# The second half of a decode kernel's result accumulated in another quadrant of the PE array

## The chip, the cores and the metric

The kernel runs on one core of one Trainium2 chip. The metric is the device time of one execution in microseconds (us). Three runs of the kernel before took 129.09 to 129.24 us, the median is 129.13 us. One further execution was recorded by the hardware profiler; all lines of profile come from such executions. Engines are named as in the profile: PE is TensorE (PEld its weight loads), DVE is VectorE, ACT ScalarE, POOL GpSimd, and SPq the queue of SyncE, which issues the large DMA transfers.

## The reference

One token (a row `x` of 576 values) goes through a parallel block: attention over a sliding window of a cache, and a gated MLP, both on the normalised row, and both added to `x`:

```python
def _A_ref(x, k_cache, v_cache, wq, wo):
    W = min(4096, max(256, Sk // 4))                     # 4096
    q = (x @ wq) ...                                     # 32 heads of 128
    k = jnp.repeat(k_cache[:, :, Sk - W:, :], rep, axis=1)   # 16 kv heads, rep = 2
    v = jnp.repeat(v_cache[:, :, Sk - W:, :], rep, axis=1)
    scores = jnp.einsum('bhqd,bhkd->bhqk', q, k) * Dh ** (-0.5)
    p = _softmax(scores, axis=-1)
    o = jnp.einsum('bhqk,bhkd->bhqd', p, v)
    return o... @ wo                                     # 4096 x 576

def _B_ref(x, w_in, w_sp, b_sp, w_out):
    z = _gelu(jnp.einsum('bsd,df->bsf', x, w_in))        # 576 x 4608
    z1 = z[..., :Fh].copy()
    z2 = _layernorm(z[..., Fh:], axis=-1)
    g = jnp.einsum('ts,bsf->btf', w_sp, z2) + b_sp[None, :, None]
    return jnp.einsum('bsf,fd->bsd', z1 * g, w_out)      # 2304 x 576

xn = _layernorm(x, axis=-1)
return x + _A_ref(xn, ...) + _B_ref(xn, ...)
```

All tensors are bf16. Some 51 MB are read: 16 heads of 4096 rows of K and of V (33.6 MB), `wq`, `w_in`, `w_out` and `wo`.

## The kernel before

All large reads are issued by SyncE at the head of the program, in the order in which they are used, into a ring of seven buffers: `wq` in two pieces, then K and V in pairs of heads with `w_in` between, then `w_out` (one piece, `wout` in the profile) and last `wo` in six pieces of 10, 8, 6, 4, 2 and 2 rows, a row being 128 x 576 values. A transfer into a buffer of the ring waits until what it held has been used; for the last pieces of `wo` that is the attention's product with V.

The order on each engine is the order of the program; no scheduler moves instructions. The steps:

- The row is normalised and spread (`XT`), and `wq` is applied in four quadrants of the PE array (L208, `qps`). A quadrant is a strip of 32 columns of the array, and it writes the corresponding 32 partitions of PSUM. `tile_position=(0, 32 * g)` chooses it. Without this argument a matmul with a single column of weights uses the strip at 0.
- For each of the 16 heads, VectorE transposes K (`kT`, L248) and TensorE makes the scores (`S`, L256). Four heads make a group, one quadrant for each head. A group's softmax (`sm_a`, `sm_b`: `mx`, `p`, `pt`, `PT`) and its product with V (`pv`, L306, into `ops`, four heads in four quadrants) come while the next group's scores are made.
- `yb` turns `ops` into the group's columns of `Y` (`om`, L316; `on`, L320; four small fp32 matmuls into `yps`, L323; the cast to `Y`, L327).
- The MLP's first half (`z_mms`, `z_rest`, `z_norm`) lies among the first groups and leaves its result in `hv`.
- The result is accumulated in two PSUM tiles `acc0` and `acc1`, 288 columns each, in a bank of their own. They are begun with `x` itself (L396, two matmuls over one row). `out_mms` (L407) adds one row of `w_out` or `wo`: for each half a weight load of one column of `hv` or `Y` and a matmul over 288 columns.

At the end of the program, behind the last product with V, stand 12 rows of `w_out`, the last group's `yb`, 6 more rows of `w_out`, and the 32 rows of `wo`. The first matmul on each piece waits for its transfer. Then VectorE casts the first half of the result (L427) and ScalarE the second (L428), both into `res`, and SyncE stores it (L429).

Of the kernel before, what the change touches and what calls it, by code (L numbers as in the profile page):

```python
# [8 lines left out]
FP32 = mybir.dt.float32  # L9
# [5 lines left out]
D = 576  # L15
# [14 lines left out]
CW = D // 2  # L30
# [9 lines left out]
def kernel(  # L40
# [14 lines left out]
    nc = tc.nc  # L55
    P = nc.NUM_PARTITIONS
# [10 lines left out]
    ps_a = ctx.enter_context(tc.tile_pool(name="ps_a", bufs=1, space=bass.MemoryType.PSUM))  # L67
    ps_b = ctx.enter_context(tc.tile_pool(name="ps_b", bufs=1, space=bass.MemoryType.PSUM))
# [45 lines left out]
    xrow = const.tile([1, D], BF16, name="xrow")  # L114
# [14 lines left out]
    ones_b = const.tile([1, P], BF16, name="ones_b")  # L129
# [28 lines left out]
    for n in range(2):  # L158
        t = ps_s.tile([P, 2, 512], FP32, name=f"S{n}")
# [46 lines left out]
    for s, wv in wq_sb:  # L206
        for g in range(4):
            nc.tensor.matmul(  # L208
                qps[32 * g:32 * g + 2, :], lhsT=XT[:, s, :], rhs=wv[:, 512 * g:512 * (g + 1)],
                start=(s == 0), stop=(s == NS - 1), tile_position=(0, 32 * g),  # L210
# [12 lines left out]
    for k in range(4):  # L223
        for be in range(4):
            nc.tensor.matmul(
                qps2[:, k, be, :].rearrange("p (r g) -> p r g", r=2),
                lhsT=q_rep[0:NR, 2 * k + be // 2, be % 2].rearrange("p a d -> p (a d)"),
                rhs=idq, start=True, stop=True)
# [14 lines left out]
    def t_head(j):  # L243
        kT = ktpool.tile([P, NT, 2, 32, 2], BF16, name=f"kT{j}", tag="kT")
        src = K[j].rearrange("p t d -> p (t d)").bitcast(FP32)
        dst = kT[:].rearrange("p t b k e -> p (t b k e)").bitcast(FP32)
        for hf in range(2):
            nc.vector.transpose(dst[:, 1024 * hf:1024 * (hf + 1)], src[:, 1024 * hf:1024 * (hf + 1)])  # L248
        KT[j] = kT

    def s_head(j):
        g, i = divmod(j, GK)
        kv = KT.pop(j)[:].rearrange("p t b k e -> p b e t k")
        for hf in range(2):
            for be in range(4):
                nc.tensor.matmul(  # L256
                    S[g % 2][32 * i:32 * i + 8, hf, :],
                    lhsT=Qb[:, j, be].rearrange("p a h -> p (a h)"),
                    rhs=kv[:, be // 2, be % 2, 16 * hf:16 * hf + 16, :],
                    start=(be == 0), stop=(be == 3), tile_position=(0, 32 * i),  # L260
                )
# [13 lines left out]
    def sm_a(g):  # L275
        s = S[g % 2]
        nc.vector.tensor_reduce(out=mx[:, 0:1], in_=s[:], op=ALU.max, axis=mybir.AxisListType.XY)  # L277
        bk = spread(mx, mb, g, ALU.max, "m")
        nm = work.tile([P, 1], FP32, name=f"nm{g}", tag="nm")
        nc.vector.tensor_scalar_mul(nm[:], bk[:, 0:1], -SCALE)  # L280
        p = work.tile([P, 1024], BF16, name=f"p{g}", tag="p")
        nc.scalar.activation(p[:], s[:].rearrange("p a n -> p (a n)"), ACT.Exp, bias=nm[:, 0:1], scale=SCALE,  # L282
                             accum_out=lx[:, 0:1])
        st[g] = {"p": p}

    def sm_b(g):
        d = st[g]
        pt = work.tile([P, NT, 32], BF16, name=f"pt{g}", tag="pt")
        nc.vector.transpose(pt[:].rearrange("p t x -> p (t x)"), d["p"][:])  # L289
        lbk = spread(lx, lb, g, ALU.add, "l")  # L290
        rs = work.tile([P, 1], FP32, name=f"rs{g}", tag="rs")
        nc.vector.reciprocal(rs[:], lbk[:, 0:1])
        PT = work.tile([P, GK, NT, 2], BF16, name=f"PT{g}", tag="PT")
        pt4 = pt[:].rearrange("p t x -> p (t x)").bitcast(FP32).rearrange("p (t x) -> p t x", x=16)
        PT4 = PT[:].rearrange("p i t h -> p (i t h)").bitcast(FP32).rearrange("p (i t) -> p i t", i=GK)
        for i in range(GK):
            for a in range(4):
                nc.scalar.copy(PT4[32 * a:32 * a + 32, i, :], pt4[32 * i:32 * i + 32, :, a])  # L298
        d["PT"] = PT
        d["rs"] = rs  # L300
# [29 lines left out]
    def z_mms():  # L330
        zps = ps_a.tile([P, 2, NF], FP32, name="zps", tag="a")
        for s, wv in win_sb:
            wt = wv.rearrange("k (p t) -> k t p", t=NF)
            for t in range(NF):
                nc.tensor.matmul(zps[:, :, t], lhsT=wt[:, t, :], rhs=XT[:, s, :],  # L335
                                 start=(s == 0 and t == 0), stop=(s == NS - 1 and t == NF - 1),
                                 skip_group_check=True)
        return zps

    def z_rest(zps):  # L340
        z = const.tile([P, 2, NF], FP32, name="z")
        nc.vector.tensor_copy(z[:], zps[:])
        u = const.tile([P, 2, NF], FP32, name="u")
        nc.vector.tensor_mul(u[:], z[:], z[:])
        nc.vector.tensor_scalar(out=u[:], in0=u[:], scalar1=0.044715, scalar2=1.0,
                                op0=ALU.mult, op1=ALU.add)
        nc.vector.tensor_mul(u[:], u[:], z[:])
        th = const.tile([P, 2, NF], FP32, name="th")
        nc.scalar.activation(th[:], u[:], ACT.Exp, scale=-2.0 * GELU_C)
        nc.vector.tensor_scalar_add(th[:], th[:], 1.0)  # L350
        nc.vector.reciprocal(th[:], th[:])
        G = const.tile([P, 2, NF], FP32, name="G")
        nc.vector.tensor_mul(G[:], th[:], z[:])
        sz = const.tile([P, 2], FP32, name="sz")
        nc.vector.reduce_sum(sz[:, 0:1], G[:, 1], axis=AXX)
        jz = const.tile([P, NF], FP32, name="jz")
        nc.vector.tensor_tensor_reduce(
            out=jz[:], in0=G[:, 1], in1=G[:, 1], scale=1.0, scalar=0.0,
            op0=ALU.mult, op1=ALU.add, accum_out=sz[:, 1:2],
        )  # L360
        return G, sz

    def z_norm(G, sz):
        psz = ps_m.tile([P, 512], FP32, name="psz", tag="m")
        nc.tensor.matmul(psz[:, 0:2], lhsT=ones_f[:], rhs=sz[:], start=True, stop=True)
        mz = const.tile([P, 4], FP32, name="mz")
        nc.vector.tensor_scalar_mul(mz[:, 0:2], psz[:, 0:2], 1.0 / FH)
        nc.vector.tensor_mul(mz[:, 2:3], mz[:, 0:1], mz[:, 0:1])
        nc.vector.tensor_sub(mz[:, 2:3], mz[:, 1:2], mz[:, 2:3])
        nc.vector.tensor_scalar_add(mz[:, 2:3], mz[:, 2:3], EPS)  # L370
        nc.gpsimd.tensor_tensor(out=mz[:, 3:4], in0=mz[:, 2:3], in1=mhalf[:], op=ALU.pow)
        zn = const.tile([P, NF], FP32, name="zn")
        nc.vector.tensor_scalar(out=zn[:], in0=G[:, 1], scalar1=mz[:, 0:1], scalar2=mz[:, 3:4],
                                op0=ALU.subtract, op1=ALU.mult)
        nc.vector.tensor_scalar(out=zn[:], in0=zn[:], scalar1=wb[:, 0:1], scalar2=wb[:, 1:2],  # L375
                                op0=ALU.mult, op1=ALU.add)
        hv = const.tile([P, NF], BF16, name="hv")
        nc.vector.tensor_mul(hv[:], G[:, 0], zn[:])
        return hv

    for j in range(HKV):
        t_head(j)
        g, o = divmod(j, GK)
        if g > 0 and o == 0:
            sm_a(g - 1)
        if g > 0 and o == 1:
            sm_b(g - 1)
        s_head(j)
        if j == GK - 1:
            zps = z_mms()  # L390
        if j == GK + 1:
            G, sz = z_rest(zps)

            acc = [ps_a.tile([1, 512], FP32, name="acc0", tag="a"), ps_b.tile([1, 512], FP32, name="acc1")]
            for n in range(2):
                nc.tensor.matmul(acc[n][:, 0:CW], lhsT=ones_b[:, 0:1], rhs=xrow[:, CW * n:CW * (n + 1)],  # L396
                                 start=True, stop=False)
        if j == GK + 2:
            hv = z_norm(G, sz)
        if g > 1 and o == 0:  # L400
            yb(g - 2)
        if g > 0 and o == 3:
            pv(g - 1)

    def out_mms(lhs, col, wv, last):
        for n in range(2):
            nc.tensor.matmul(acc[n][:, 0:CW], lhsT=lhs[:, col:col + 1], rhs=wv[:, CW * n:CW * (n + 1)],  # L407
                             start=False, stop=last)

    def out_hv(c):  # L410
        for t, wv in wout_sb[6 * c:6 * c + 6]:
            out_mms(hv, t, wv, False)
# [10 lines left out]
    for t, wv in wo_sb:  # L423
        out_mms(Y, t, wv, t == 31)

    res = const.tile([1, D], BF16, name="res")
    nc.vector.tensor_copy(res[:, 0:CW], acc[0][:, 0:CW])  # L427
    nc.scalar.copy(res[:, CW:D], acc[1][:, 0:CW])  # L428
    nc.sync.dma_start(out.flatten_outer_dims(), res[:])  # L429


# [28 lines left out]
```

## Time and profile before

| what | us |
|---|---|
| median of three runs | 129.13 |
| lowest and highest | 129.09, 129.24 |
| profiled execution | 129.18 |
| its span, first to last instruction | 127.4 |
| TensorE busy (share of the span) | 79.6 (62%) |
| VectorE busy | 74.0 (58%) |
| ScalarE busy | 23.3 (18%) |
| output matmuls on `wo` (64), busy together, each | 8.0, 0.286 |
| output matmuls on `wout` (36), busy together, each | 4.6, 0.286 |

50.96 MB are read from memory, 400 GB/s over the span. The mean granted clock of TensorE is 0.786 of full speed. In the page's rows of slices, each digit is a fortieth of the span (3.2 us) in tenths; in rows of groups, the numbers behind the bar are busy time in us, the mean duration of one instruction in ns, and the idle time before them. Matmuls are pipelined, so the starts of two may be closer than the duration of one.

### The profile page before, as it was taken

How to read it: one execution, taken by the hardware profiler on the slowest of the kernel's cores; microseconds unless marked ns; L12 is line 12 of the kernel's file. 1: busy time of each engine (PE TensorE's matmuls, PEld its weight loads, DVE VectorE, ACT ScalarE, POOL GpSimd, SP SyncE). 2: the span in 40 equal slices, each digit the busy share in tenths (PEclk: the TensorE clock that was granted, in tenths of full speed). 3: DMA queues.
4: the chain of work that ended last, by engine and by line, in shares of the span. 5: the costliest groups of instructions: out<-in, count | busy, mean ns of one | idle time of the engine just before them, and what ended most of it. 6: DMA issues, size and time to landing. Idle time of an engine off the chain costs nothing.

```text
span 127.4 us, 1582 instructions
## 1 busy us (share of the span) xinstructions
PE 79.6 (62%) x610; PEld 37.2 (29%) x610; DVE 74.0 (58%) x155; ACT 23.3 (18%) x77; POOL 3.6 (3%) x19
## 2 busy tenths in 40 slices
PE   0002911599999697509179653995579703889992
PEld 0001301133899512002123210232112201247660
DVE  6704147999000599463598699998999656050001
ACT  1200030000000003920000307403074059000001
POOL 4301000000000000000100000000000000000000
PEclk9999995558975555555955999679769995599999
DMA  4999999999999999999999999999999999999920
GB/s 135 437 416 427 412 427 432 443 434 421 434 408 432 422 419 430 427 430 427 427 430 427 430 427 430 422 424 430 427 427 430 424 461 452 396 408 429 407 107 0
DMA packets 6174, 51.04 MB, mean 401 GB/s; under 512 B 534, under 2 KB 536, under 8 KB 1048
## 3 DMA queue, kind: packets, MB, share of 16 engines
q1 hardware_dynamic: 6082, 50.96, 94.9%
q8 instruction: 4, 0.07, 0.2%
q10 hardware_dynamic: 86, 0.00, 0.0%
q14 instruction: 2, 0.02, 0.0%
HBM read 50.96 MB, written 0.00 MB: 400 GB/s over the span
## 4 chain that ended last, share of the span: by engine, by line
issue 40%; DMA 27%; PE 21%; DVE 9%; POOLq 0%; POOL 0%; ACT 0%; SPq 0%
DMA wout<-in_B_w_out_dram 20%; PE acc L407 10%; PE S L256 7%; DMA x<-in_A_x_dram 7%; DVE kT L248 4%; PE ops L306 3%; DVE pt L289 1%; DVE on L320 1%; DVE om L316 1%; PE ps_x L185 0%; POOLq L455 0%; PE yps L323 0%; POOL mv L191 0%; ACT res L428 0%; DVE zn L375 0%
## 5 line engine op out<-in xcount | busy, mean ns | idle before, releaser
L256 PE MATMUL S<-kT,Qb 128*8 128x512 bf16 x128 | 42.0, 507 | 20.9 <-DVE kT L248 20.3
L248 DVE STREAM_TRANSPOSE kT<-k 128x1024 f32<-128x1024 f32 x32 | 37.0, 1212 | 11.2 <-DMA k<-in_A_k_cache_dram 11.2
L256 PEld LDWEIGHTS <-Qb 128*8 128x8 bf16 x128 | 12.1, 101 | 46.6 <-issue 38.9
L298 ACT COPY PT<-pt 32x32 f32<-32x32 f32 x64 | 15.4, 241 | 14.3 <-DVE pt L289 13.4
L306 PE MATMUL ops<-v,PT 128*8 128x512 bf16 x128 | 15.0, 497 | 0.4 <-ACT PT L298 0.4
L282 ACT ACTIVATE p<-S,nm 128x1024 bf16<-128x1024 f32 x4 | 4.5, 1114 | 54.5 <-DVE nm L280 54.5
L335 PEld LDWEIGHTS <-win 128*128 128x128 bf16 x162 | 10.1, 171 | 0.4 <-issue 0.4
L335 PE MATMUL zps<-XT,win 128*128 128x2 bf16 x162 | 10.2, 202 | 0.0
L407 PE MATMUL acc<-wo,Y 128*1 128x288 bf16 x64 | 8.0, 286 | 0.0
L323 PE MATMUL yps<-on,sel 128*32 128x32 f32 x32 | 1.9, 209 | 8.5 <-DVE on L320 8.5
L306 PEld LDWEIGHTS <-PT 128*8 128x8 bf16 x128 | 4.4, 93 | 6.5 <-issue 3.7
L407 PEld LDWEIGHTS <-Y 128*1 128x1 bf16 x64 | 5.4, 84 | 2.5
L175 PE MATMUL ps_x<-x,rmat 64*128 64x9 bf16 x1 | 0.2, 165 | 9.4 <-DMA x<-in_A_x_dram 9.4
L277 DVE TENSOR_REDUCE mx<-S 128x1 f32<-128x1024 f32 x4 | 4.9, 1214 | 1.4 <-PE S L256 1.4
L316 DVE SCALAR_TENSOR_TENSOR om<-ops,rs,dmask 128x512 f32<-128x512 f32 x4 | 3.0, 744 | 4.6 <-PE ops L306 4.6
L427 DVE CAST res<-acc 1x288 bf16<-1x288 f32 x1 | 0.4, 447 | 8.9 <-PE acc L407 8.9
L289 DVE STREAM_TRANSPOSE pt<-p 128x1024 bf16<-128x1024 bf16 x4 | 4.8, 1210 | 1.4 <-ACT p L282 1.4
L407 PE MATMUL acc<-wout,hv 128*1 128x288 bf16 x36 | 4.6, 286 | 0.6 <-DMA wout<-in_B_w_out_dram 0.6
L323 PEld LDWEIGHTS yps<-on,sel 128*32 128x32 f32 x32 | 1.5, 122 | 10.0 <-DVE on L320 8.4
L320 DVE TENSOR_REDUCE on<-om 128x128 f32<-128x512 f32 x4 | 4.1, 1024 | 0.1
L208 PE MATMUL qps<-wq,XT 128*2 128x512 bf16 x36 | 3.5, 561 | 0.7 <-DVE XT L199 0.7
L407 PEld LDWEIGHTS <-hv 128*1 128x1 bf16 x36 | 3.1, 85 | 2.4 <-issue 1.2
(89 smaller groups left out, 35.5 us busy)
## 6 DMA issues: line engine op xcount, KB each, us to landing
k<-in_A_k_cache_dram SPq DMA_DIRECT2D x8, 2048.0 KB, 23.5
v<-in_A_v_cache_dram SPq DMA_DIRECT2D x8, 2048.0 KB, 20.5
win<-in_B_w_in_dram SPq DMA_DIRECT2D x3, 1728.0 KB, 22.4
wout<-in_B_w_out_dram SPq DMA_DIRECT2D x1, 2592.0 KB, 25.7
wq<-in_A_wq_dram SPq DMA_DIRECT2D x1, 2560.0 KB, 8.7
wq<-in_A_wq_dram SPq DMA_DIRECT2D x1, 2048.0 KB, 12.9
wo<-in_A_wo_dram SPq DMA_DIRECT2D x1, 1440.0 KB
wo<-in_A_wo_dram SPq DMA_DIRECT2D x1, 1152.0 KB
```

What stands on the lines that cost most here:

```text
L208: nc.tensor.matmul(qps[32 * g:32 * g + 2, :], lhsT=XT[:, s, :], rhs=wv[:, 512 * g:512 * (g + 1)], start=(s == 0), stop=(s == NS - 1), tile ...
L248: nc.vector.transpose(dst[:, 1024 * hf:1024 * (hf + 1)], src[:, 1024 * hf:1024 * (hf + 1)])
L256: nc.tensor.matmul(S[g % 2][32 * i:32 * i + 8, hf, :], lhsT=Qb[:, j, be].rearrange("p a h -> p (a h)"), rhs=kv[:, be // 2, be % 2, 16 * hf ...
L277: nc.vector.tensor_reduce(out=mx[:, 0:1], in_=s[:], op=ALU.max, axis=mybir.AxisListType.XY)
L282: nc.scalar.activation(p[:], s[:].rearrange("p a n -> p (a n)"), ACT.Exp, bias=nm[:, 0:1], scale=SCALE, accum_out=lx[:, 0:1])
L289: nc.vector.transpose(pt[:].rearrange("p t x -> p (t x)"), d["p"][:])
L298: nc.scalar.copy(PT4[32 * a:32 * a + 32, i, :], pt4[32 * i:32 * i + 32, :, a])
L306: nc.tensor.matmul(ops[32 * i:32 * i + 8, :], lhsT=d["PT"][:, i, 4 * tb:4 * tb + 4, :].rearrange("p t h -> p (t h)"), rhs=V[GK * g + i][:, ...
L316: nc.vector.scalar_tensor_tensor(out=om[:].rearrange("p c d -> p (c d)"), in0=ops[:], scalar=d["rs"][:, 0:1], in1=dmask[:].rearrange("p c ...
L320: nc.vector.reduce_sum(on[:], om[:].rearrange("p c d -> p d c"), axis=AXX)
L335: nc.tensor.matmul(zps[:, :, t], lhsT=wt[:, t, :], rhs=XT[:, s, :], start=(s == 0 and t == 0), stop=(s == NS - 1 and t == NF - 1), skip_gr ...
L407: nc.tensor.matmul(acc[n][:, 0:CW], lhsT=lhs[:, col:col + 1], rhs=wv[:, CW * n:CW * (n + 1)], start=False, stop=last)
```

## The change

The two accumulator tiles get all 128 partitions instead of one. The first half still uses row 0 of its tile, the second half row 32 of its own, and every matmul into them names its quadrant: `tile_position=(0, 0)` for the first half and `(0, 32)` for the second. The banks, the number of instructions, their order on each engine and their waits stay as they were. The two casts at the end read the rows where the halves now stand; ScalarE's reads partition 32 and writes partition 0.

```diff
@@ -391,10 +391,12 @@
         if j == GK + 1:
             G, sz = z_rest(zps)
 
-            acc = [ps_a.tile([1, 512], FP32, name="acc0", tag="a"), ps_b.tile([1, 512], FP32, name="acc1")]
-            for n in range(2):
-                nc.tensor.matmul(acc[n][:, 0:CW], lhsT=ones_b[:, 0:1], rhs=xrow[:, CW * n:CW * (n + 1)],
-                                 start=True, stop=False)
+            acc = []
+            for n, pool in enumerate((ps_a, ps_b)):
+                t = pool.tile([P, 512], FP32, name=f"acc{n}", tag="ab"[n])
+                acc.append(t[32 * n:32 * n + 1, 0:CW])
+                nc.tensor.matmul(acc[n], lhsT=ones_b[:, 0:1], rhs=xrow[:, CW * n:CW * (n + 1)],
+                                 start=True, stop=False, tile_position=(0, 32 * n))
@@ -404,8 +406,8 @@
     def out_mms(lhs, col, wv, last):
         for n in range(2):
-            nc.tensor.matmul(acc[n][:, 0:CW], lhsT=lhs[:, col:col + 1], rhs=wv[:, CW * n:CW * (n + 1)],
-                             start=False, stop=last)
+            nc.tensor.matmul(acc[n], lhsT=lhs[:, col:col + 1], rhs=wv[:, CW * n:CW * (n + 1)],
+                             start=False, stop=last, tile_position=(0, 32 * n))
@@ -424,8 +426,8 @@
     res = const.tile([1, D], BF16, name="res")
-    nc.vector.tensor_copy(res[:, 0:CW], acc[0][:, 0:CW])
-    nc.scalar.copy(res[:, CW:D], acc[1][:, 0:CW])
+    nc.vector.tensor_copy(res[:, 0:CW], acc[0])
+    nc.scalar.copy(res[:, CW:D], acc[1])
     nc.sync.dma_start(out.flatten_outer_dims(), res[:])
```

## The prediction

> **What bounds the kernel now.** I read the page's span and slices first, then the chain of waits for the tail, then the output matmuls, the issues of the weight `wo`, and last the reading of the result.
>
> ```profile
> span 127.4 us, 1582 instructions
> PEclk9999995558975555555955999679769995599999
> DMA  4999999999999999999999999999999999999920
> ```
>
> The DMA engines are full until the last two or three slices of 3.2 us, so transfers bound everything up to about 122 us. What the change can touch is what comes after the last byte. The chain of waits from 110 us on:
>
> ```profile
> 112.44 0.04 issue
> 112.49 2.67 PE acc L407 x21
> 115.35 9.56 PE acc L407 x78
> 124.93 0.39 ACT res L428
> ```
>
> Here the reader sees that from the landing of `wout` (112.44) to the copy of the result the chain is TensorE alone: 100 output matmuls (18 rows of `wout`, 32 rows of `wo`, two halves each), one behind the other. The page's groups give their price:
>
> ```profile
> L407 PE MATMUL acc<-wo,Y 128*1 128x288 bf16 x64 | 8.0, 286 | 0.0
> L407 PEld LDWEIGHTS <-Y 128*1 128x1 bf16 x64 | 5.4, 84 | 2.5
> ```
>
> One lasts 286 ns, but 64 take 8.0 us: (8.0 - 0.286)/63 = 0.1225 us from start to start, 0.245 us per row. They run from 116.89 to 124.89. The 84 ns weight loads are hidden beside them. Next, when `wo` is there (issues of SyncE, then the time to landing):
>
> ```profile
> 101.10 0.81 SPq L93 DMA_DIRECT2D wo<-in_A_wo_dram  x2
> 111.74 0.80 SPq L93 DMA_DIRECT2D wo<-in_A_wo_dram  x2
> DMA to landing us min/median/max: 11.1/11.3/20.6
> ```
>
> The fourth piece (rows 24 to 27) is issued at about 101.5 and lands 20.6 later, 122.1. The fifth and sixth (two rows each) are issued at 111.74 and 112.16 and land at 122.84 and 123.46. That is 0.34 us per row. Counting back by it, the first three pieces (10, 8 and 6 rows) land at about 116.0, 118.7 and 120.7. Each is there before its rows' turn now: row 30 is reached at 116.89 + 60 x 0.1225 = 124.24, when its data has lain there for 0.8 us. So TensorE, not DMA, ends the kernel, but with little in hand.
>
> **The change: two streams in place of one.** The same matmuls, loads and copies remain, in the same order on every engine; only the array columns of the second half move, from quadrant 0 to quadrant 1. Nothing is added to a queue, no wait is added, and SyncE's loads wait for `ops`, `kT` and earlier transfers, never for `acc`, so no transfer moves. The question is whether two streams in different quadrants run at once. The product with V does so already, where it overlaps the end of the scores of a head in the fourth quadrant (timeline of TensorE at full clock):
>
> ```profile
> 98.70 0.39 PE L256 MATMUL S<-kT,Qb 128*8 128x512 bf16 x1
> 98.71 0.39 PE L306 MATMUL ops<-v,PT 128*8 128x512 bf16 x3
> 98.93 0.38 PE L256 MATMUL S<-kT,Qb 128*8 128x512 bf16 x1
> 98.94 0.39 PE L306 MATMUL ops<-v,PT 128*8 128x512 bf16 x3
> ```
>
> Four matmuls of 512 columns, each with its own data, start within 0.01 us, and the next four 0.22 to 0.23 us later: 0.055 us for a load and a matmul. One of the four (`S`) writes another bank than the other three, so neither quadrants nor banks hold each other up. A row of the output is two such pairs; its price is bounded by 0.1225 (fully parallel) and 0.245 us (serial as now). I take 0.1225, since the 0.055 per pair seen here is below the 0.061 that this needs.
>
> Step 1, `wout`: the first 12 rows start at 112.49 and are through at 112.49 + 12 x 0.1225 = 113.96 instead of 115.4. `on` ends at 113.76 (L320), so the eight small matmuls of `yps` (0.4 us, another quadrant) still don't wait. The last six rows end by about 114.9. The cast of `Y` came 0.3 us after `yps` and took 0.2; it ends at about 115.0, later than `wout` now, but before the data: the cover is the first piece of `wo`, not there until 116.0. Without it the cast would cost some 0.1 us.
>
> Step 2, `wo`: now a chase of the transfers. Rows 0 to 9 run from 116.0 to 117.2; rows 10 to 17 wait for 118.7, the next six for 120.7, the next four for 122.1, then 122.84. Each piece is done before the next lands. The last two rows start at 123.46 + 0.05 (the gap that `wout` shows, 112.44 to 112.49) = 123.51; the second starts 0.12 later and lasts 0.29, so the last matmul ends at 123.92 instead of 124.89: 0.97 us gained. The other 3.0 us of the 32 x 0.1225 saved turn into waits for DMA.
>
> Step 3, the clock. These waits leave TensorE 40% busy, and the clock may be halved. Stretches of 3.41 us in which the clock was constant (TensorE busy time, clock, DMA):
>
> ```profile
> 56.86:60.27 3.41, 2.81 (x7) 0.50 1.01 428
> 70.50:73.92 3.42, 1.84 (x18) 1.00 1.01 429
> 77.33:80.75 3.42, 1.43 (x6) 1.00 1.01 422
> 80.75:84.16 3.41, 3.41 (x19) 0.50 1.00 425
> ```
>
> After 1.84 us busy the clock stayed at 1.0; after 1.43 it fell to 0.5; after 2.81 at half clock it rose again. On this grid the stretch 114.88 to 118.29 would have 10 x 0.1225 + 0.16 = 1.4 busy, so I expect half clock from 118.29. There a row takes 0.24 (288 of the 512 columns that took 0.43 in L256 at half clock), the stretch to 121.70 is busy for some 2.9 us, and the clock is back at 121.70, in time for the last pieces. Cost: nothing, covered by the wait for 122.1 and 122.84. If the phase of the grid falls otherwise and half clock lasts to the end, rows 18 to 23 run 120.8 to 122.2, the next six rows follow without a gap to 123.7, and the last row starts at 123.9 and lasts 0.42 (the same shape at half clock took 0.39 to 0.44 in the two `xrow` matmuls), ending at 124.33: 0.41 of the 0.97 is lost. Bounds: 0 and 0.41. I take 0.
>
> Against the clock's fall stands the Trainium skill, "TensorE: Matmul & The Clock Gate", section "HAM oscillation": only idle gaps above about 3.4 us are to be avoided. By it the gaps here, 1.5 us at most, would keep full clock, and the end would be that of step 2. The trace disagrees: the stretch that ended at 80.75 held no gap above 2.2 us.
>
> Step 4, the reading.
>
> ```profile
> 124.81 0.45 DVE L427 CAST res<-acc 1x288 bf16<-1x288 f32 x1 [8.92 <-PE acc L407]
> 124.93 0.39 ACT L428 CAST res<-acc 1x288 bf16<-1x288 f32 x1 [16.34 <-PE acc L407]
> 125.35 0.31 SPq L429 DMA_DIRECT2D out_dram<-res  x1
> ```
>
> Now VectorE has a head start of 0.12 on ScalarE, as its half is done one matmul earlier. With both halves ending together both start at 123.96, and VectorE (0.45) is last, at 124.41 against 124.35. SyncE issued 0.09 after VectorE's end and 0.03 after ScalarE's; between these I take 0.09, so the store goes at 124.50 instead of 125.35. That ScalarE's copy reads partition 32 and writes partition 0 I cost at nothing: L298 does the like 64 times (241 ns). At the outside it costs what that row would, 0.24.
>
> Sum: 0.97 - 0.12 = 0.85 us. The profiled execution took 129.18 (span 127.4, 1.78 around it), so 128.33; it was 0.05 above the median, so 128.3 by the median. With half clock at the end 128.7.
>
> **The rivals.**
> *No parallelism.* Two streams of one column of weights each might still be served in turn. The row stays at 0.245, every gate stays covered, the last matmul ends at 124.89: 129.1. The L306 lines speak against it; for it, only that no line here runs exactly two quadrants with 288 columns.
>
> *Weight loads come into the open* (slower). If loads for alternating quadrants could not run ahead, each row would cost two loads and a stream, 2 x 0.084 + 0.1225 = 0.29. From 112.49, 50 rows: the last starts 49 x 0.29 later, 126.7, and ends at 127.0; plus 0.1 for the reading, 2.2 us above now: 131.3. It decides from 0.247 per row up: 112.49 + 49 x 0.247 + 0.29 = 124.9 is today's end. Against it: the same 0.084 loads hide within one quadrant now, and in L306 they do at 0.055 per pair.
>
> For this rival speaks the same page, section "Part 3: Packing small matmuls": a weight load overlaps a running matmul only where the row groups differ, and here all rows are the same. By that rule the sum would be that of the rival; the hidden loads of today's rows, all on the same 128 rows, contradict it.
>
> **How the numbers follow.** Parallel with full clock at the end 0.60, at 128.3 (128.1 to 128.5: the spread of the runs, 0.15, and 0.06 for SyncE's step). Parallel with half clock at the end 0.23, at 128.5 to 128.8. No parallelism 0.09. Open weight loads 0.08. A measurement of this kernel tells 0.2%, 0.26 us, from no change, so the first two are faster: 0.83. The range 128.1 to 129.0 covers both with a margin for the landing of the last piece and the ScalarE copy; the last two lie outside.
>
> **What would show it.** Right: the 64 `wo` matmuls in pairs of near-equal starts; TensorE idle before each piece, ended by DMA `wo`; the last piece landing near 123.5 as now; the chain naming a transfer of `wo` in place of L407; VectorE, not ScalarE, last. Wrong: 64 matmuls in 8.0 us without gaps, a row above 0.247 us, or a last landing that itself has moved, for which I have no mechanism.

## The result and the profile after

The changed kernel takes 128.34 us in the median of 7 runs (128.13 to 129.0), the kernel before 129.35 in the 7 runs beside it (129.09 to 129.89). The ratio is 0.992 with a 95% interval of 0.990 to 0.995: faster by 0.8%. The profiled executions took 128.45 and 129.18 us, with spans of 126.6 and 127.4.

The page of the changed kernel, span and slices:

```profile
span 126.6 us, 1582 instructions
PEclk9999998559995555875556995599655798559999
DMA  4999999999999999999999999999999999999950
```

The transfers fill the same time as before, but the span now ends closer behind them. The clock's pattern (`PEclk`) differs from that before from the seventh slice on; how far that reaches the end is told below, under steps 1 and 3. The chain of waits from 110 us on (start, duration, what):

```profile
109.92 2.99 PE ops L306 x13
112.91 0.03 issue
112.94 10.55 DMA wo<-in_A_wo_dram
123.49 0.04 issue
123.53 0.45 PE acc L409 x4
123.98 0.43 DVE res L429
```

Of 100 output matmuls four are left on the chain. What ends the kernel is the landing of the last two rows of `wo`, then two pairs of matmuls (L409 is the L407 of before), then VectorE's cast. The piece of 10.55 us is not the price of that transfer alone: it was issued 0.78 us later than before (112.94 against 112.16, since the product with V ended a microsecond later in this execution) and still landed at 123.5. So the issue did not set the landing; that the transfers ahead of it did is the likely reading, which no run here tried.

The groups on `wo`, then the timeline of TensorE over them:

```profile
L409 PE MATMUL acc<-wo,Y 128*1 128x288 bf16 x64 | 4.9, 285 | 3.2 <-DMA wo<-in_A_wo_dram 3.0
L409 PEld LDWEIGHTS <-Y 128*1 128x1 bf16 x64 | 2.8, 82 | 5.3 <-issue 4.4
```

```profile
115.98 1.39 PE L409 MATMUL acc<-wo,Y 128*1 128x288 bf16 x20
118.72 1.15 PE L409 MATMUL acc<-wo,Y 128*1 128x288 bf16 x16 [1.35 <-DMA wo<-in_A_wo_dram]
120.78 0.90 PE L409 MATMUL acc<-wo,Y 128*1 128x288 bf16 x12 [0.92 <-DMA wo<-in_A_wo_dram]
122.17 1.10 PE L409 MATMUL acc<-wo,Y 128*1 128x288 bf16 x12 [0.48 <-DMA wo<-in_A_wo_dram]
123.53 0.41 PE L409 MATMUL acc<-wo,Y 128*1 128x288 bf16 x4 [0.27 <-DMA wo<-in_A_wo_dram]
```

One matmul lasts as long as before (285 ns), and 20 of them, ten rows, take 1.39 us: (1.39 - 0.285)/9 = 0.123 us per row, where it was 0.245. The two of a row start 0.003 us apart in the trace. In the last column stand 3.0 us of waits for `wo`, of which there were none: most of the 3.9 us that the pairs saved on `wo` was turned into them. The end of the page's work:

```profile
123.97 0.45 DVE L429 CAST res<-acc 1x288 bf16<-1x288 f32 x1 [8.48 <-PE acc L409]
124.01 0.39 ACT L430 CAST res<-acc 1x288 bf16<-1x288 f32 x1 [14.74 <-PE acc L409]
124.50 0.32 SPq L431 DMA_DIRECT2D out_dram<-res  x1
```

Both casts start together, VectorE's ends last, and the store goes at 124.50 instead of 125.35: 0.85 us earlier.

### The profile page after: what moved, and what is told of

The parts are those of the page before. It is cut to its first block, busy times and chain, and to the rows that moved or that the text cites. A ratio compares the mean times of both kernels' runs of the same rounds, so it can differ in the third digit from the quotient of the medians.

```text
span 126.6 us, 1582 instructions
## 1 busy us (share of the span) xinstructions
PE 76.2 (60%) x610; PEld 33.7 (27%) x610; DVE 74.0 (58%) x155; ACT 23.3 (18%) x77; POOL 3.6 (3%) x19
## 4 chain that ended last, share of the span: by engine, by line
issue 41%; DVE 25%; DMA 15%; PE 12%; ACT 4%; POOLq 0%; POOL 0%; ACTq 0%
DVE kT L248 11%; DMA wo<-in_A_wo_dram 8%; PE S L256 7%; DMA x<-in_A_x_dram 7%; ACT PT L298 3%; PE ops L306 3%; DVE mx L277 3%; DVE pt L289 3%; DVE on L320 2%; DVE om L316 1%; ACT p L282 1%; PE yps L323 1%; DVE mt L266 1%; DVE mb L272 1%; PE ps_x L185 0%
## 5 line engine op out<-in xcount | busy, mean ns | idle before, releaser
L256 PE MATMUL S<-kT,Qb 128*8 128x512 bf16 x128 | 43.4, 532 | 19.6 <-DVE kT L248 19.2
L306 PE MATMUL ops<-v,PT 128*8 128x512 bf16 x128 | 14.3, 478 | 0.4 <-ACT PT L298 0.4
L409 PE MATMUL acc<-wo,Y 128*1 128x288 bf16 x64 | 4.9, 285 | 3.2 <-DMA wo<-in_A_wo_dram 3.0
L306 PEld LDWEIGHTS <-PT 128*8 128x8 bf16 x128 | 4.1, 91 | 6.3 <-issue 3.0
L208 PE MATMUL qps<-wq,XT 128*2 128x512 bf16 x36 | 4.0, 627 | 0.8 <-DVE XT L199 0.8
L409 PEld LDWEIGHTS <-Y 128*1 128x1 bf16 x64 | 2.8, 82 | 5.3 <-issue 4.4
L219 DVE CAST q_rep<-qps 128x512 bf16<-128x512 f32 x2 | 1.4, 692 | 4.6 <-PE qps L208 3.9
L217 ACT CAST q_rep<-qps 128x512 bf16<-128x512 f32 x2 | 1.2, 586 | 14.6 <-DVE q_rep L219 14.6
```

The costliest lines, as they stand in the source:

```text
L256: nc.tensor.matmul(S[g % 2][32 * i:32 * i + 8, hf, :], lhsT=Qb[:, j, be].rearrange("p a h -> p (a h)"), rhs=kv[:, be // 2, be % 2, 16 * hf ...
L306: nc.tensor.matmul(ops[32 * i:32 * i + 8, :], lhsT=d["PT"][:, i, 4 * tb:4 * tb + 4, :].rearrange("p t h -> p (t h)"), rhs=V[GK * g + i][:, ...
L409: nc.tensor.matmul(acc[n], lhsT=lhs[:, col:col + 1], rhs=wv[:, CW * n:CW * (n + 1)], start=False, stop=last, tile_position=(0, 32 * n))
```

## The experiments

The theory after this reading: two streams run at once because they are in different quadrants, and the end is now the last landing plus what waits for it. The rivals: that something else in the edit (new tiles, explicit positions, banks) made the gain, and that TensorE's own rate still sets the end.

**Both halves in the same quadrant, all else as changed.**

```diff
-                acc.append(t[32 * n:32 * n + 1, 0:CW])
+                acc.append(t[32:33, 0:CW])
...
-                                 start=True, stop=False, tile_position=(0, 32 * n))
+                                 start=True, stop=False, tile_position=(0, 32))
...
-                             start=False, stop=last, tile_position=(0, 32 * n))
+                             start=False, stop=last, tile_position=(0, 32))
```

> The changed kernel with both halves in quadrant 1 (each still in its own bank, new tiles and explicit positions kept). Theory (two streams run at once only because they are in different quadrants): back to one stream, the 64 wo matmuls busy 7.9 to 8.0 us without gaps, 0.1225 us from start to start, the last one ending near 124.9, the time that of the kernel before (ratio 0.998 to 1.002). Rival (the gain comes from the tiles or the explicit positions, not from the separation): two starts 0.003 us apart as in the changed kernel, busy 4.9 us, ratio near 0.992.

Measured: 129.33 us against 129.42, ratio 0.9998 (0.9975 to 1.0021). Its group and its last chain:

```profile
L409 PE MATMUL acc<-wo,Y 128*1 128x288 bf16 x64 | 8.0, 286 | 0.0
115.24 9.56 PE acc L409 x78
124.83 0.39 ACT res L430
```

Eight microseconds without a gap, and the last 78 matmuls one behind the other, as before the change. The whole gain hangs on the second quadrant: the new tiles, the explicit positions and two banks give nothing without it. Which quadrant a single stream uses makes no difference.

**Both halves in one bank, two quadrants.**

```diff
-            for n, pool in enumerate((ps_a, ps_b)):
-                t = pool.tile([P, 512], FP32, name=f"acc{n}", tag="ab"[n])
+            t = ps_a.tile([P, 512], FP32, name="acc0", tag="a")
+            for n in range(2):
                 acc.append(t[32 * n:32 * n + 1, 0:CW])
```

> The changed kernel with both halves in one tile and bank, rows 0 and 32 of it. Theory (the quadrant alone matters): as the changed kernel, pairs 0.1225 us apart, ratio to the kernel before near 0.992. Rival (two streams need banks of their own): pairs serialise, 0.245 us per row, ratio near 1.000. A smaller cost could come from the two casts reading one bank at once: up to 0.4 us if they take turns.

Measured: 128.77 us, ratio 0.9961 (0.9937 to 0.9986). The group and the casts:

```profile
L409 PE MATMUL acc<-wo,Y 128*1 128x288 bf16 x64 | 4.9, 285 | 4.2 <-DMA wo<-in_A_wo_dram 4.1
123.77 0.45 DVE L429 CAST res<-acc 1x288 bf16<-1x288 f32 x1 [9.56 <-PE acc L409]
124.25 0.39 ACT L430 CAST res<-acc 1x288 bf16<-1x288 f32 x1 [15.81 <-DVE res L429]
124.67 0.31 SPq L431 DMA_DIRECT2D out_dram<-res  x1
```

The streams run side by side in one bank as in two, so the rival that they need banks of their own fell. But ScalarE's cast now waits for VectorE's (the releaser in its bracket), where in the changed kernel both started together; the one difference is that both now read one tile, in one bank, and which of the two makes the wait was not tried. The store goes 1.39 us after the last landing (123.28) where it was 1.01 in the changed kernel: 0.38 lost. That is the smaller cost that the expectation named, and about what the ratio is short of 0.992 by, though the two intervals overlap. So 0.38 of the 0.85 us by which the changed kernel's store came sooner hangs on the separate tiles and banks, by way of the reading alone. Whether the two reads could safely go at once without that wait was not tried.

**Four rows instead of two behind the last landing, with two streams and with one.**

```diff
-    for n in (10, 8, 6, 4, 2, 2):
+    for n in (10, 8, 6, 2, 2, 4):
```

> The changed kernel with wo in pieces of 10, 8, 6, 2, 2, 4 rows, so that four rows instead of two wait for the last landing. Theory (the end is the last landing plus what waits for it): the last landing stays at 123.4 to 123.6, two more rows at 0.1225 come behind it, the end and the time grow by 0.25 us (ratio to the kernel before near 0.994). Rival (TensorE's own work sets the end): no change, 0.992.

> The kernel before with wo in pieces of 10, 8, 6, 2, 2, 4 rows. Theory (there TensorE's stream sets the end and the landings are covered): row 28 is reached at 123.75, after the last landing near 123.5, so nothing moves: ratio 0.998 to 1.002. Rival (landings already set the end before): slower by up to 0.5 us, two rows at 0.245, ratio 1.004.

Measured: with two streams 128.73 us, ratio 0.994 (0.992 to 0.996); with one 129.34, ratio 0.9987 (0.9966 to 1.0007). The first ratio is the expected one, but its interval overlaps with that of the change (0.990 to 0.995), so the time alone does not tell the two apart; the chain does. With two streams:

```profile
123.49 0.04 issue
123.53 0.70 PE acc L409 x8
124.23 0.43 DVE res L429
```

and with one:

```profile
115.57 9.56 PE acc L407 x78
125.15 0.39 ACT res L428
```

With two streams the landing stood still at 123.49, and behind it eight matmuls took 0.70 us where four had taken 0.45. With one stream the last 78 matmuls still run one behind the other, and the time did not move. So TensorE set the end before, and the last landing sets it now, both as the theory has it.

**No waits for `wo` at all.** The 32 rows of `Y` are multiplied by rows of `wout`, which is already there, while `wo` is loaded as ever.

```diff
-    for t, wv in wo_sb:
-        out_mms(Y, t, wv, t == 31)
+    for t, _ in wo_sb:
+        out_mms(Y, t, wout_sb[t % NF][1], t == 31)
```

> The changed kernel with the 32 rows of Y multiplied by rows of wout, which is already there, in place of wo; wo is still loaded, so the transfers are the same and only TensorE's waits for wo go (the result is not the reference's). Theory: 32 rows at 0.1225 us without gaps, the 64 matmuls busy 4.0 to 4.2 us (3.92 plus one latency), ended near 119.5 to 120; the kernel can't end before wo has landed at 123.5, and the end follows the last landing by the 1 us or more of closing work: 126.0 to 127.5, against 128.3 for the changed kernel. Rival (two quadrants stream slower than 0.1225 when nothing gates them, for loads or data): busy above 4.5 us.

> The kernel before with the same replacement of wo's rows by wout's, one stream. Theory (landings of wo were covered): nothing moves, 64 matmuls busy 8.0 us, ratio 0.998 to 1.002. Rival (a wait for wo was hidden in the stream): faster by more than 0.3 us.

Measured: with two streams 126.05 us (125.98 to 126.18), ratio 0.975 (0.974 to 0.977); with one 129.24, ratio 0.9993 (0.9981 to 1.0005). With two streams:

```profile
L409 PE MATMUL acc<-wout,Y 128*1 128x288 bf16 x64 | 4.1, 286 | 0.0
119.45 0.32 SPq L431 DMA_DIRECT2D out_dram<-res  x1
DMA to landing us min/median/max: 11.6/11.9/20.8
```

and with one:

```profile
L407 PE MATMUL acc<-wout,Y 128*1 128x288 bf16 x64 | 8.0, 286 | 0.0
```

Left to themselves two streams take 4.1 us where one takes 8.0, which is half the time per row ((4.1 - 0.286)/31 = 0.123). The last matmul ended at 118.90, sooner than the 119.5 to 120 expected. The result is on its way at 119.45, yet the span ends at 124.2, 0.8 us after the last landing of `wo` (the last issue, 111.52, plus 11.9 is 123.4). With TensorE's waits for `wo` gone, the transfers alone hold the end there, so this is about the floor of this order of transfers. The changed kernel stands 2.3 us above it: two pairs of matmuls, a cast and a store that must follow the last byte. With one stream it makes no difference whether `wo` has landed: its landings were covered.

**One row behind the last landing.**

```diff
-    for n in (10, 8, 6, 4, 2, 2):
+    for n in (10, 8, 6, 4, 3, 1):
```

> The changed kernel with wo in pieces of 10, 8, 6, 4, 3, 1 rows: one row instead of two behind the last landing. Theory: the end comes 0.12 us sooner, last matmul ending 0.33 after the last landing instead of 0.45, ratio to the kernel before near 0.991. Rival (a small last transfer lands later, since its fixed part weighs more): the landing moves by as much or more, no gain.

Measured: 128.17 us, ratio 0.9919 (0.9904 to 0.9934). The last four rows, and the store:

```profile
123.25 0.66 PE L409 MATMUL acc<-wo,Y 128*1 128x288 bf16 x8 [0.40 <-DMA wo<-in_A_wo_dram]
124.46 0.31 SPq L431 DMA_DIRECT2D out_dram<-res  x1
```

The last two landings came at 123.21 and 123.57 in the trace, and the last matmul ended at 123.90, 0.33 behind the last landing, as expected. The store went 0.89 behind it, 0.12 less than in the changed kernel. But that landing was 0.08 later than in the changed kernel's profile, and the ratio cannot be told from the change's own (0.992). It is the fastest of the variants that compute the whole result, by no margin that these runs can show.

## Why the prediction was right

**The bound.** It said that transfers end at about 123.5 and that TensorE alone runs behind them, with 0.8 us in hand at row 30. The two variants with one stream (longer last piece, no waits) did not move, which is what that reading demands.

**Two streams.** It took 0.1225 us per row from the four-quadrant matmuls of L306, against 0.245. Measured 0.123, both gated and ungated. The rivals of no parallelism and of open weight loads fell with that: the loads of 82 ns stay beside the matmuls. The second quadrant is the cause of the doubled rate, by the variant with one quadrant and that with one bank.

**Step 1, `wout`.** Nothing of it reached the end, as predicted, but the cover was not the one that the prediction names. The product with V before and after, then what followed it after the change:

```profile
108.64 3.27 PE L306 MATMUL ops<-v,PT 128*8 128x512 bf16 x29 [0.40 <-ACT PT L298]
```

```profile
109.32 3.58 PE L306 MATMUL ops<-v,PT 128*8 128x512 bf16 x29 [0.40 <-ACT PT L298]
114.82 0.34 PE L323 MATMUL yps<-on,sel 128*32 128x32 f32 x5 [0.33 <-DVE on L320]
115.09 0.78 PE L409 MATMUL acc<-wout,hv 128*1 128x288 bf16 x10
```

The product started 0.68 us later and took 0.31 longer at half clock, and `on` came a microsecond later with it, so `yps` did wait for `on`, 0.33 us. The late start is hardly the change's doing: of the matmuls ahead of it only the two over `xrow` differ, and in the other profiles it lies anywhere between 108.22 (two streams) and 109.18 (one stream). The prediction had the last rows of `wout` end by 114.9 and the cast of `Y` at 115.0; they ended at 115.87 and 115.49, and the first piece of `wo` landed at 115.94. Of the 1 us of cover that the prediction counted on, 0.07 was left. What it overlooked is a second cover: the wait of 1.35 us for the second piece would have taken up a delay of the first ten rows as well, so its 0.1 us for an uncovered cast was a price for nothing.

**Step 2, the chase.** Last matmul predicted to end at 123.92, measured 123.94; waits for `wo` predicted 3.0 us, measured 3.0. The last landing did not move.

**Step 3, the clock.** Predicted: half clock from about 118.3 to 121.7, at no cost. In the profile of the changed kernel it did not fall there, as its grid of 3.41 us lay elsewhere; in those of the longer last piece and of the one row it did. The stretches of the changed kernel, then those of the longer last piece (start and end, length, busy time, clock):

```profile
113.31:116.72 3.41, 2.96 (x54) 1.00 1.00 424
116.72:120.14 3.42, 1.80 (x28) 1.00 1.00 418
120.14:123.55 3.41, 1.98 (x26) 1.00 0.53 210
```

```profile
115.05:118.46 3.41, 1.39 (x20) 1.00 0.98 414
118.46:121.88 3.42, 3.25 (x28) 0.50 0.95 381
121.88:125.29 3.41, 1.43 (x20) 1.00 0.11 41
```

1.80 and 1.98 us busy kept the clock, 1.39 lost it for the next stretch, and 3.25 at half clock brought it back. That agrees with what the prediction read from the kernel before (kept at 1.84, lost at 1.43, back at 2.81). Between 1.43 and 1.80, though, busy time does not decide. The variant with one bank:

```profile
114.37:117.78 3.41, 1.66 (x26) 1.00 1.00 422
117.78:121.20 3.42, 1.86 (x28) 1.00 1.00 410
121.20:124.61 3.41, 1.66 (x20) 1.00 0.22 84
```

Its first 1.66 us kept the clock; after its second, from 124.61 on, it was 0.50. The two stretches differ in their matmuls, 26 and 20. What the clock goes by stays open. In the longer last piece rows at half clock started 0.24 us apart, as predicted, and the waits covered it: the last pieces ran at full clock. In that variant's stretch from 115.05 no gap was longer than 1.35 us, and the clock fell behind it. So the Trainium skill's rule in "TensorE: Matmul & The Clock Gate", section "HAM oscillation", that only idle gaps above about 3.4 us need care, did not hold there. Half clock in the last rows, priced at 0.41, was seen in no profile here, so its share of the runs stays open. That price rests on 0.42 us for a matmul at half clock, read from the two `xrow` matmuls; these work on one partition and the output matmuls on 128, so the shape is not the same. The output matmuls at half clock took up to 0.448 us.

**Step 4, the reading.** Predicted 124.50 for the store, measured 124.50, with VectorE last, by 0.02 us. ScalarE's copy from partition 32 to partition 0 took 389 ns against 387: no cost.

**The sum.** 0.85 us predicted; the store goes 0.85 us earlier, the profiled executions differ by 0.73 and the medians of the shared runs by 1.0. The interval of the ratio leaves 0.65 to 1.3 us, and 0.85 lies in it. Predicted 128.3, measured 128.34: that these agree so closely is in part luck. The prediction counted from a median of 129.13; from the 129.35 of the runs beside, the same 0.85 would have given 128.5. What is confirmed is the steps, not the last digit.

## What to carry to other kernels

Here matmuls with one column of weights and 288 columns of data, one behind the other in one strip of the array, started 0.1225 us apart; alternating them between two strips halved the time of a row, without a change to any data. What that is worth is not the time saved. Of 3.9 us saved on `wo`, 0.97 reached the end of the stream and the rest became waits for transfers; 0.12 of the 0.97 then went to a cast that lost its head start. Before such a change, count back from the last landing, then size what stands behind it: each row behind it here now costs 0.12 us, and a cast that must wait for the other 0.4.

## What the runs showed of the hardware

The first point is that here matmuls of different strips did not start in the order of the program. In the kernel before, 24 output matmuls stand ahead of the eight of `yps`, which use the fourth strip. The timeline has only 21 of them ahead of the first `yps`:

```profile
112.49 2.73 PE L407 MATMUL acc<-wout,hv 128*1 128x288 bf16 x21 [0.58 <-DMA wout<-in_B_w_out_dram]
114.94 0.31 PE L323 MATMUL yps<-on,sel 128*32 128x32 f32 x4
115.06 0.29 PE L407 MATMUL acc<-wout,hv 128*1 128x288 bf16 x1
```

The 22nd starts 0.12 us after the first `yps`. That fits strips that are fed separately; no run here set out to prove it.

The second is a landing that did not follow its issue: the last two rows of `wo`, issued at 112.16 in the one execution and at 112.94 in the other, landed within 0.05 us of each other.

The third is how the stream of transfers ends. In the kernel before, the mean busy share of the 16 DMA engines falls from 1.00 (120 to 121 us) to 0.64 in the next microsecond and 0.25 in the one after, and the last landing comes at 123.5. So the last two microseconds before it are carried by a part of the engines; no run here asked why.
